# Pairs 5 to 11 of a gated linear attention with an MLP behind it: y laid out by tokens and turned by DMA, q and k turned in four transfers a pair, and a new order of all steps

## The chip, the cores and the metric

The kernel runs on one core of one Trainium2 chip. Its five engines have short names in the profile: PE is TensorE (PEld is its weight load), DVE is VectorE, ACT is ScalarE, POOL is GpSimd and SP is SyncE, which here only issues DMA transfers. The metric is the time of one execution on the device in microseconds (us). All times of the kernel before are from three runs and from one profiled execution.

## The reference, cut to what matters

First a gated linear attention, for 4 batches of 8 heads, 768 tokens each and 48 elements a head, then an MLP over all 3072 tokens with the activation h * cos(h):

```python
f = 1 / (1 + exp(-f_logit))                                  # all inputs (4, 8, 768, 48)
for t in range(S):
    state = f[:, :, t, :, None] * state + einsum('bhd,bhe->bhde', k[:, :, t], v[:, :, t])
    y[:, :, t] = einsum('bhd,bhde->bhe', q[:, :, t], state)
x = y.transpose(0, 2, 1, 3).reshape(3072, 384)
h = x @ w_in                                                 # w_in (384, 2048)
out = (h * cos(h)) @ w_out                                   # w_out (2048, 384)
```

## The kernel before, in words

**Pairs.** The attention is done in chunks of 128 tokens, and two chunks of a batch make a pair: 12 pairs, three to a batch, so pairs 0, 3, 6 and 9 begin a batch with an empty state. A pair's inputs f, k, q and v come in with tokens on the partitions (two neighbouring tokens to a partition, counted by e). Each pair runs these steps, with the pair's number in the name: `ex`, `ln`, `fx`, `fy` (ACT, logarithm of the gate), `qa`, `ka`, `ad` (POOL or DVE, one token folded into its neighbour), `cum` (PE, sums along the chunk), `eb`, `ei` (ACT, their exponentials), `qm` and `km` (q and k times these, into the tile `qk`), `vb` and `vt` (copies of v), then

- `tq`, `tk`: q and k are turned so that their elements lie on the partitions. In pairs 0 to 4 PE turns them (L435) and DVE or ACT copies the result out as `qkt`. In pairs 5 to 11 (`TURN_QK`) there is one DMA transpose for each half of the heads (L424), issued by SP: two a pair, 128 x 1024 elements each.
- `sc` (PE, L456): scores of q against k; `am` (DVE, L461): masked and copied to `am`.
- `ps` (PE, L479): k times v; `st` and `sz` (DVE): the carried state.
- `y` and `yi` (PE, L531): masked scores times v, and q times the carried state. They are made with the 384 outputs on the partitions, in strips of 32, so that the result is already the transposed x that the MLP reads: 32 matmuls of 32 columns of weights and 128 moving columns for `y`, and 24 for `yi` (12 in the first pair of a batch).
- `xe.0`, `xe.1` (ACT or DVE, L197): the two chunks of y copied from PSUM to the tile `x`.

**MLP.** Unit 0 and unit 1 are the two chunks of pair 0, and unit n + 1 is pair n, 256 tokens wide. A unit has steps `h` (PE, L579; h7.21 is unit 7, column block 2, half 1), `co` (ACT, the cosine), `g` (DVE, the product, L561), then for each 128 rows of the output four steps `o` (PE, L595), `ot` (copy) and `out` (DMA).

**Weights.** Eight transfers `w0.0` to `w0.3` (w_in) and `w1.0` to `w1.3` (w_out) of 768 KB, each cast to bfloat16 by a step `wc` on POOL or ACT.

**Order.** The order of all steps is written out by hand in the string `ORDER`: each word is a step, the letter of its engine (T PE, S ACT, V DVE, G POOL, Y SP) and the buffers that it takes. Every engine does its steps in this order, so a step that waits holds up all steps of its engine behind it; SP's queue is one list for loads, transposes and outputs. Steps `zf` are matmuls of zeros that keep PE busy in the beginning; other steps that begin with z clear buffers.

Of the kernel before, what the change touches and what calls it, by code (L numbers as in the profile page):

```python
# [38 lines left out]
fx0.0:S ei0.1:S0 fx0.1:S ei0.0:S ka0.0:V f1.1:Y1 km0.0:G0 f1.0:Y ex1.1:S ka0.1:V zf10:T2 zf11:T2
zf12:T2 zf13:T2 zf14:T2 zf15:T2 zf16:T2 zf17:T2 tk0.0:T2 eb0.1:S0 ex1.0:S ln1.1:S1 ln1.0:S fx1.0:S  # L40
q0.1:Y0 q0.0:Y v0:Y0 fx1.1:S eb0.0:S qa0.1:V zqk.1:V qm0.1:V vb0:S0 f3:Y2 k1.1:Y1 km0.1:V qa0.0:V
zf18:T3 cum1.1:T3 zf19:T4 zf20:T4 zf21:T4 tq0.1:T0 cum1.0:T1 qm0.0:G zsz.2:G eb1.0:S1 vt0.3:S2
k1.0:Y ei1.0:S0 ex3:S zf22:T4 zf23:T4 zf24:T4 zf25:T4 zf26:T4 ps0.1:T4,5 ps0.0:T tk0.1:T v1:Y1 f2:Y0
qkt0.1:V0 eb1.1:S ln3:S0 ei1.1:S ka1.0:G q1.0:Y0 tq0.0:T ka1.1:G km1.1:G0 zvt.1:G vt0.0:S ad3:G1
vt0.1:G q1.1:Y vb1:S1 qkt0.0:V1 vt0.2:G zsz.1:G ex2:S w0.1:Y0 w0.0:Y1 k3:Y0 q3:Y1 w0.3:Y2 ln2:S1
vt1.2:S1 fy3:S zf27:T6 zf28:T6 zf29:T6 zf30:T6 zf31:T6 zf32:T6 sc0.0:T0 sz0.01:V2 sz0.00:V w0.2:Y3
ad2:G0 vt1.0:G km1.0:V vt1.3:G wc0.1:G am0.0:V0 zf33:T6 zf34:T6 yi0:T4 sc0.1:T2 am0.1:V1 st0.11:V
sz0.11:V3 wc0.0:G k2:Y1 zf35:T6 zf36:T6 zf37:T6 zf38:T6 ps1.1:T6,7 tk1.0:T0 ps1.0:T zf39:T1 zf40:T1
zf41:T1 cum3:T1 fy2:S ei3:S0 fx3:S ka3:G eb3:S2 vt1.1:S fx2:S km3.0:G1 qa3:G qm3.0:G km3.1:G qm3.1:G
w1.0:Y0 qa1.0:V st0.10:V qa1.1:V qm1.0:V wc0.2:G ka2:G q2:Y2 tk1.1:T2 zf42:T3 zf43:T3 y0:T3 tq1.0:T  # L50
xe0.1:S0 sz0.10:V st1.00:V st1.01:V qm1.1:V v2:Y1 zf44:T5 zf45:T5 zf46:T5 zf47:T5 zf48:T5 tq1.1:T
cum2:T1 sz1.00:V1 qkt1.0:V0 eb2:S0 xe0.0:S ei2:S1 qkt1.1:V1 km2.0:G0 km2.1:G zf49:T5 sc1.0:T4
sz1.01:V zf50:T0 zf51:T0 sc1.1:T2 h0.01:T0 st1.11:V sz1.11:V2 am1.1:V0 wc1.0:G qa2:G zf52:T6 zf53:T6
h0.00:T co0.0:S0 qm2.1:G am1.0:V1 h1.01:T2 h1.00:T co1.0:S1 y1:T6,4 yi1:T g0.0:V1 xe1.1:V1 st1.10:V
qm2.0:G vb2:G1 sz1.10:V g1.0:V4 w1.2:Y3 xe1.0:S tk3.0:T5 h2.01:T0 tq3.0:T w1.3:Y0 qkt3.0:V0 v3:Y0
f4:Y0 h2.10:T6 h2.00:T sc3.0:T4 tq3.1:T2 tk3.1:T h2.11:T wc1.2:G wc1.3:G vt2.1:G1 wc0.3:S vb3:G0
co2.0:S1 am3.0:V0 g2.0:V2 h2.20:T4 h2.21:T h0.11:T0 co2.1:S0 qkt3.1:S1 co2.2:S1 sc3.1:T2 w1.1:Y3
g2.1:V am3.1:V1 g2.2:V h0.10:T h1.11:T6 h1.10:T h2.30:T2 tk2.1:T4 tk2.0:T5 co0.1:S0 co1.1:S2 g0.1:V
g1.1:V h2.31:T o2.0:T0 co2.3:S0 tq2.1:T vt3.2:G2 vt3.1:G tq2.0:T o0.0:T1 o3.0:T6 o1.0:T7 qkt2.0:S2
vt2.0:S g2.3:V qkt2.1:V3 sc2.0:T2 ex4:S o3.2:T o0.2:T am2.0:V2 ln4:S1 ps2.0:T4 sc2.1:T2 vt2.3:G  # L60
ps2.1:T am2.1:V3 st2.01:V st2.00:V sz2.01:V1 sz2.00:V wc1.1:S f5:Y2 ex5:S ln5:S0 o1.2:T o2.3:T
o3.3:T o0.3:T o2.2:T q4:Y2 ps3.0:T4,5 ps3.1:T zsz.0:G vt2.2:G ad4:G0 yi2:T2,3 y2:T vt3.3:G sz3.01:V0
sz3.00:V o1.3:T cum4:T4 v4:Y0 vt3.0:G ad5:G0 fy4:S eb4:S0 st3.11:V fx4:S k4:Y1 fy5:S qa4:G qm4.0:G1
fx5:S ei4:S1 o0.1:T o2.1:T o3.1:T xe2.0:V1 st3.10:V sz3.10:V1 qm4.1:G sz3.11:V xe2.1:V ot2:V0
h3.00:T2 o1.1:T cum5:T0 ei5:S0 eb5:S2 k5:Y0 h3.01:T ot0:V1 vb4:G0 ka4:G y3:T4,5 yi3:T q5:Y1 h3.10:T0
h3.11:T co3.0:S0 xe3.0:V0 xe3.1:V ot1:V2 ot3:V3 co3.1:S2 g3.0:V4 h3.21:T4 h3.20:T co3.2:S1 h4.21:T6
h4.20:T g3.1:V ka5:G km4.0:G co4.2:S0 km4.1:G vt4.1:G2 qa5:G h4.11:T2 h4.10:T g3.2:V co4.1:S2
h4.31:T0 k6:Y2 qm5.1:G0 h4.30:T vt4.0:G vt4.2:G km5.1:G f6:Y1 v5:Y0 v6:Y1 f7:Y0 tq4.0:T4 tq4.1:T5
out3:Y tk4.0:T tk4.1:T co4.3:S1 g4.2:V2 h3.31:T6 h3.30:T qkt4.1:S0 qkt4.0:V1 g4.1:V o5.1:T4 co3.3:S0
o5.2:T o5.0:T o4.1:T5 g4.3:V g3.3:V ps4.1:T0,1 ps4.0:T st4.01:V st4.00:V sc4.1:T2 sc4.0:T6 am4.1:V0  # L70
am4.0:V1 sz4.00:V0 sz4.01:V qm5.0:G vt4.3:G st4.10:V tq5.1:Y2 sz4.10:V2 o5.3:T o4.2:T km5.0:G o4.0:T
o4.3:T ex6:S ln6:S0 vb6:G0 ad6:G0 ex7:S cum6:T2 y4:T3,6 tq5.0:Y3 yi4:T ot5:S3 st4.11:V sz4.11:V
# [30 lines left out]
h9.20:T0 h9.21:T g9.0:V g9.1:V h10.10:T4 tq10.1:Y1 co9.2:S2 out7:Y g9.2:V h10.00:T2 h10.11:T
h10.20:T6 vt11.3:S1 co10.1:S1 g10.1:V4 h10.01:T co10.0:S2 o16.1:T0 h10.21:T o16.0:T g10.0:V o16.2:T
o16.3:T sc10.0:T2 co10.2:S1 out13:Y ot16:S3 g10.2:V sc10.1:T4 ps11.1:T1 vt11.0:G vt10.3:G2 ps11.0:T
qa11:G vt11.1:S qm11.1:G st11.01:V tq11.1:Y2 sz11.01:V2 am10.0:V0 am10.1:V1 h10.31:T6 o17.3:T0
# [611 lines left out]
```

## Time and profile before

| | |
|---|---|
| median of 3 runs | 183.1 us (183.05 to 183.54) |
| span of the profiled execution | 180.9 us |
| PE, PEld busy | 172.6, 123.9 us |
| DVE, ACT, POOL busy | 134.6, 130.7, 109.2 us |
| bytes moved by DMA | 33.93 MB |

The span runs from the first to the last instruction of the profiled execution. Its own time is this span of 180.9 us and what lies around it, which the span does not show; the median of the runs is 2.2 us above the span. Busy times of PE are of pipelined matmuls that overlap, so the distance from the start of one matmul to the start of the next, as the chain of waits and the timeline give it, is what one costs.

### The profile page before, as it was taken

The page shows a single profiled execution, that of the slowest core. Times are in us where ns is not written, and L with a number is a line of the kernel's source. Part 1 is how long each engine was busy: PE and PEld are TensorE (multiplying, and loading weights), DVE is VectorE, ACT ScalarE, POOL GpSimd, SP SyncE. Part 2 cuts the span into 40 slices and gives each one's busy share as a digit, 9 for nine tenths or more (in the row PEclk, how much of TensorE's full clock was granted, in tenths as well). Part 3 has the DMA queues.
Part 4 walks back from the last instruction along what each step waited for, and adds up shares of the span by engine and source line. Part 5 has one row for each costly group of instructions (what it writes and reads, how often), then busy time and mean ns, then how long its engine had stood idle before and what let it go on. Part 6 is the DMA issues. An engine that isn't in the chain of part 4 may idle for free.

```text
span 180.9 us, 5814 instructions
## 1 busy us (share of the span) xinstructions
PE 172.6 (95%) x2460; PEld 123.9 (69%) x2464; DVE 134.6 (74%) x206; ACT 130.7 (72%) x187; POOL 109.2 (60%) x139
## 2 busy tenths in 40 slices
PE   7899789999999999999999999999999999999992
PEld 2455467785668977778667886658788767787651
DVE  5259988897595988897999697689888894356260
ACT  3985987777878899989997899769768452473221
POOL 4229899999969986989665977890798000000000
PEclk9999999999999999999999999999999999999999
DMA  5999999999999944986899999559927500110313
GB/s 149 261 261 276 343 320 341 250 318 284 301 265 233 274 83 123 252 210 145 122 180 308 173 267 278 124 131 251 203 92 182 100 4 0 43 47 4 130 43 131
DMA packets 72282, 33.93 MB, mean 188 GB/s; under 512 B 65344, under 2 KB 70720, under 8 KB 72256
## 3 DMA queue, kind: packets, MB, share of 16 engines
q1 hardware_dynamic: 71584, 33.27, 75.7%
q8 instruction: 19, 0.31, 0.7%
q10 hardware_dynamic: 672, 0.30, 0.6%
q14 instruction: 7, 0.06, 0.1%
HBM read 25.17 MB, written 4.72 MB: 165 GB/s over the span
## 4 chain that ended last, share of the span: by engine, by line
PE 81%; DMA 7%; ACT 3%; DVE 3%; SPq 2%; issue 1%; ACTq 0%
PE ps L595 35%; PE ps L579 33%; PE ps L531 5%; DMA f<-in_f_logit_dram 4%; PE ps L456 4%; DMA v<-in_v_dram 3%; SPq L296 2%; PE ps L479 2%; DVE g L561 1%; PE ps L435 1%; PE ps L374 1%; DVE am L461 1%; PE ps L264 1%; ACT f L344 0%; ACT f L329 0%
## 5 line engine op out<-in xcount | busy, mean ns | idle before, releaser
L561 DVE TENSOR_TENSOR g<-ps,co 128x1024 bf16<-128x1024 f32 x48 | 57.4, 1220 | 18.0 <-ACT co L584 16.7
L595 PE MATMUL ps<-w_out_bf,g 128*128 128x384 bf16 x384 | 68.9, 326 | 0.0
L579 PE MATMUL ps<-x,w_in_bf 128*128 128x256 bf16 (+1 forms) x624 | 68.1, 264 | 0.5 <-DVE x L197 0.4
L584 ACT ACTIVATE co<-ps,halfpi 128x1024 bf16<-128x1024 f32 x48 | 52.7, 1113 | 19.8 <-PE ps L579 19.5
L579 PEld LDWEIGHTS <-w_in_bf 128*128 128x128 bf16 x624 | 56.3, 98 | 9.2 <-DVE x L197 0.6
L595 PEld LDWEIGHTS <-g 128*128 128x128 bf16 x384 | 36.1, 98 | 21.4
L461 DVE TENSOR_TENSOR am<-ps,pmask 128x1024 bf16<-128x1024 f32 x24 | 28.7, 1218 | 5.2 <-PE ps L456 4.9
L404 POOL TENSOR_TENSOR qk<-k,bi 128x384 bf16<-128x384 f32 x22 | 22.0, 1008 | 5.4 <-ACT bi L391 4.7
L404 POOL TENSOR_TENSOR qk<-q,b 128x384 bf16<-128x384 f32 x21 | 20.8, 1000 | 2.7 <-DVE q L338 2.1
L197 POOL COPY vt<-vb 64x384 bf16<-64x384 bf16 x33 | 16.7, 507 | 1.6
L264 PE MATMUL ps<-zero 128*128 128x512 bf16 x50 | 14.6, 412 | 1.5 <-DVE zero L203 1.2
L503 DVE TENSOR_TENSOR sz<-ps,b 64x192 bf16<-64x192 f32 x40 | 14.1, 354 | 2.5 <-PE ps L479 1.6
L363 POOL TENSOR_TENSOR sp<-ls 128x384 bf16<-128x384 f32 x10 | 10.3, 1028 | 7.8 <-ACT ls L333 6.1
L341 POOL TENSOR_TENSOR q<-f,q 128x384 f32<-128x384 f32 x10 | 10.0, 998 | 8.0 <-DMA q<-in_q_dram 5.8
L329 ACT ACTIVATE f<-f 128x768 f32<-128x768 f32 (+1 forms) x14 | 10.4, 746 | 4.4 <-DMA f<-in_f_logit_dram 4.4
L497 DVE TENSOR_TENSOR ps<-ps,sz 64x192 f32<-64x192 f32 x32 | 11.7, 367 | 2.2 <-PE ps L479 1.1
L351 POOL TENSOR_TENSOR k<-k,f 128x384 f32<-128x384 f32 (+1 forms) x12 | 11.1, 931 | 3.4 <-DMA k<-in_k_dram 3.4
L197 ACT COPY ot<-ps 128x384 f32<-128x384 f32 (+1 forms) x14 | 6.1, 453 | 8.7 <-PE ps L595 8.7
L197 ACT CAST x<-ps 128x384 bf16<-128x384 f32 x12 | 5.5, 479 | 6.0 <-PE ps L531 6.0
L456 PE MATMUL ps<-qkt 48*64 48x128 bf16 (+1 forms) x304 | 8.7, 218 | 1.1 <-ACT x L197 0.8
L197 DVE CAST x<-ps 128x384 bf16<-128x384 f32 x12 | 6.4, 553 | 4.1 <-PE ps L531 3.9
L264 PEld LDWEIGHTS <-zero 128*128 128x128 bf16 x54 | 4.8, 103 | 5.9 <-issue 1.9
(64 smaller groups left out, 167.2 us busy)
## 6 DMA issues: line engine op xcount, KB each, us to landing
v<-in_v_dram SPq DMA_DIRECT2D x12, 384.0 KB, 5.9
out_dram<-ot SPq DMA_DIRECT2D x22, 192.0 KB, 2.3
f<-in_f_logit_dram SPq DMA_DIRECT2D x10, 384.0 KB, 6.0
...
```

The source lines that it names most:

```text
L197: (nc.scalar.copy if e == "ACT" else eng(e).tensor_copy)(out=o, in_=i)
L264: G.step(f"zf{i}", ("PE",), lambda e, dump=dump: nc.tensor.matmul(dump.ap, lhsT=zero[:, 0:128], rhs=zero, start=True, stop=True), writes=[ ...
L351: eng(e).tensor_mul(out=w.ap[:, :, 0, :], in0=w.ap[:, :, 0, :], in1=t.ap[:, :, 0, :])
L404: G.step(f"{nm}{n}.{u}", ("POOL", "DVE") if cut else ("POOL",), lambda e, u=u, j=j, src=src, dec=dec: eng(e).tensor_mul(out=qkp[u][j].ap[: ...
L456: nc.tensor.matmul(o[t0:t1, r, 2 * a + g, :].rearrange("p (e n) -> p e n", e=2), lhsT=wide[s, t0 // 64, :] if turned else wide[s].rearrang ...
L461: G.step(f"am{n}.{u}", ("DVE",), lambda e, u=u, sc=sc: nc.vector.tensor_mul(out=am[u].ap.rearrange("p r b n -> p (r b) n"), in0=sc.ap.rear ...
L497: nc.vector.tensor_add(out=view()[s], in0=view()[s], in1=S0.ap[s, :, r, :])
L503: eng(e).tensor_mul(out=new.ap[s, :, r, :].rearrange("p (u a) n -> p u a n", u=2), in0=view()[s].rearrange("p (u a) n -> p u a n", u=2), i ...
L561: nc.vector.tensor_mul(out=o.rearrange("p b (n e) -> p b n e", e=2), in0=ph.ap.rearrange("p (b e n) -> p b n e", e=2, n=64), in1=co.ap.rea ...
L579: nc.tensor.matmul(ph.ap[:, i * T:(i + 1) * T].rearrange("p (g t) -> p g t", t=C), lhsT=w_in_bf[:, kk, f0:f0 + 128], rhs=xa[:, :, kk, :], ...
L584: G.step(f"co{m}.{j}", ("ACT",), lambda e, ph=ph, co=co: nc.scalar.activation(out=co.ap, in_=ph.ap, func=AF.Sin, bias=halfpi), reads=[ph], ...
L595: nc.tensor.matmul(po.ap[:, 0:DM], lhsT=gT.ap[:, j, i * C:(i + 1) * C], rhs=w_out_bf[:, j, :], start=(po.first and j == 4 * s), stop=(po.f ...
```

## The change

The kernel's steps for pairs 0 to 4 compute what they computed. In pairs 5 to 11:

- `y` and `yi` are made with tokens on the partitions (`inner_t`, `inter_t`): 16 matmuls of 128 columns of weights (`am`) and 48 moving columns (`vt`), and 8 (4 in the first pair of a batch) of 128 columns of weights (`qkt`) and 96 moving columns (the state).
- `xe` copies the chunk to a new tile `xr` (three buffers), and a new step `tx`, a DMA transpose of 128 x 384 elements on SP's queue, writes it to `x`: two a pair.
- `tq` becomes four DMA transposes a pair, each of 64 partitions of `qk`, so that q lies in `qkt` as the weights of `inter_t` need it. For this `qm` is written in another order, by two POOL instructions of 128 x 192 elements where there was one of 128 x 384.
- `ORDER` is new as a whole. Four more `zf` steps are in it.

```diff
+TURN_X = range(5, 12)
 SLOTS = {"f": 3, "k": 3, "q": 3, "v": 3, "sp": 3, "ls": 2, "b": 3, "bi": 3, "qk": 3, "vb": 3, "vt": 3, "qkt": 5, "am": 4,
-         "sz": 4, "x": 4, "g": 5, "co": 4, "ot": 4}
+         "sz": 4, "x": 4, "xr": 3, "g": 5, "co": 4, "ot": 4}
-ZEROS = 54
+ZEROS = 58
...
+        def scaled(e, u, j, src, dec):
+            o, d = qkp[u][j].ap, dec.ap[:, 0:HB].rearrange("p (h d) -> p h d", d=D)
+            if j == 1 or n not in TURN_QK:
+                eng(e).tensor_mul(out=o[:, :, :, 0:D], in0=swap(src.ap), in1=d[:, None].broadcast_to([128, 2, 4, D]))
+                return
+            for a in range(2):
+                h = slice(2 * a, 2 * a + 2)
+                eng(e).tensor_mul(out=o[:, a, :, 0:D].rearrange("p (e r) d -> p e r d", e=2), in0=swap(src.ap[:, h]),
+                                  in1=d[:, None, h].broadcast_to([128, 2, 2, D]))
...
             if turned:
-                G.step(f"tq{n}.{u}", ("SP",), lambda e, u=u: nc.sync.dma_start_transpose(
-                    out=qkt[u].ap.rearrange("p (b n) -> p b n", n=C),
-                    in_=qk.ap[:, u].rearrange("p j e h d -> p (j e h d)")),
-                    reads=[qkp[u][0], qkp[u][1]], writes=[qkt[u]])
+                for g in range(2):
+                    G.step(f"tq{n}.{u}{g}", ("SP",), lambda e, u=u, g=g: nc.sync.dma_start_transpose(
+                        out=qkt[u].ap[:, 512 * g:512 * g + 512].rearrange("p (b n) -> p b n", n=64),
+                        in_=qk.ap[64 * g:64 * g + 64, u].rearrange("p j e h d -> p (j e h d)")),
+                        reads=[qkp[u][0], qkp[u][1]], writes=[qktg[u][g]])
                 continue
...
+        def inner_t(e):
+            for g in range(2):
+                for h in range(H):
+                    nc.tensor.matmul(py[g].ap[:, D * h:D * h + D], lhsT=am[h // 4].ap[:, h % 2, h % 4 // 2 * 2 + g, :],
+                                     rhs=vt.ap[:, H * g + h, 16:16 + D], start=(py[g].first and h == 0),
+                                     stop=(py[g].final and h == H - 1))
+
+        def inter_t(e):
+            for g in range(2):
+                if before[g] is not None:
+                    for i in range(H // 2):
+                        nc.tensor.matmul(py[g].ap[:, 2 * D * i:2 * D * i + 2 * D],
+                                         lhsT=turn(i // 2, 0)[:, i % 2, g].rearrange("p e n -> p (e n)"),
+                                         rhs=before[g].ap[:, i].rearrange("p r d -> p (r d)"),
+                                         start=(py[g].first and i == 0), stop=(py[g].final and i == H // 2 - 1))
...
+            if laid:
+                xr = Val(xrS)
+                G.step(f"xe{n}.{g}", ("ACT", "DVE"), lambda e, g=g, xr=xr: copy(e, xr.ap, py[g].ap[:, 0:DM]),
+                       reads=[py[g]], writes=[xr])
+                G.step(f"tx{n}.{g}", ("SP",), lambda e, g=g, xr=xr: nc.sync.dma_start_transpose(
+                    out=xg[g].ap, in_=xr.ap), reads=[xr], writes=[xg[g]])
+                continue
```

Of the new order, four places that the prediction speaks of. The first transfers, before and after (f0.0 is ACT's, the others SP's):

```
before  f0.1 f0.0 k0.0 k0.1 f1.1 f1.0 q0.1 q0.0 v0 f3 k1.1 k1.0 v1 f2 q1.0 q1.1 w0.1 w0.0 k3 q3 w0.3 w0.2 k2 w1.0 q2 v2 w1.2 w1.3
after   f0.0 f0.1 v0 q0.1 f1.1 k0.0 k0.1 k1.1 f1.0 q0.0 q1.1 f3 v1 f2 q1.0 k1.0 w0.1 k3 w0.0 q3 w0.2 w0.3 w1.2 k2 q2 w1.0 v2 v3
```

PE from the last steps of pair 1 on, without zf:

```
before  y0 tq1.0 tq1.1 cum2 sc1.0 sc1.1 h0.01 h0.00 h1.01 h1.00 y1 yi1 tk3.0 h2.01 tq3.0 h2.10 h2.00 sc3.0 tq3.1 tk3.1 h2.11
after   tk1.0 sc1.1 tq1.0 cum3 cum2 sc1.0 y0 yi1 y1 yi0 h0.01 h0.00 h1.00 h1.01 tk3.0 h2.00 tq3.1 tk3.1 tq3.0 h2.11
```

In the order after, DVE from the end of pair 1's loads: km1.0, qkt1.1, st1.00, st1.01, am1.1, sz1.00, sz1.01, am1.0, st1.11, xe0.0, xe1.0, xe0.1; ACT: wc0.0, co0.0.

The steps of pair 7 around its turn, and the end:

```
after   ... yi7:T y7:T xe7.1:V tx7.1:Y xe7.0:V ot9:V tx7.0:Y ...   PE from y7 to h8.21: h6.01 h6.31 h6.30 h7.31 h7.20 h7.30 h7.10 h7.21
before  ... o23.1:T ot23.0:S out23.0:Y ot23.1:S out23.1:S
after   ... o22.3:T ot22.0:S out22.0:S ot22.1:S out22.1:Y
```

More of the change, by code (lines that the diff above doesn't have):

```diff
@@ L39 @@
[L39 to L72, printed above, removed]
@@ L103 @@
[L103 to L106, printed above, removed]
-h10.30:T vt10.2:G vt10.0:G o17.2:T o17.0:T o17.1:T vt10.1:S co10.3:S1 vt11.2:S ot17:S1 g10.3:V
-yi10:T4,5 y10:T qm11.0:G tq11.0:Y3 sc11.0:T6 sc11.1:T2 xe10.1:S2 zvt.0:V st11.00:V xe10.0:V o18.0:T0
@@ new lines @@
+zf18:T3 zf19:T3 zf20:T3 zf21:T3 zf22:T3 zf23:T3 zf24:T3 zf25:T3 cum1.1:T3 ei0.0:S0 ei0.1:S eb0.1:S1
+ei1.1:S1 eb1.1:S0 zsz.0:V ka0.0:V km0.0:V0 zf26:T0 zf27:T0 zf28:T0 zf29:T0 zf30:T0 zf31:T0 tk0.0:T3
+qm0.1:G k1.1:Y0 km0.1:V zf32:T0 zf33:T0 zf34:T0 zf35:T0 tk0.1:T5 f1.0:Y ex1.0:S q0.0:Y zsz.3:G
+qa0.0:V zvt.1:G ln1.0:S tq0.1:T qkt0.1:V0 q1.1:Y1 qa1.1:V ps0.1:T1,6 zf36:T0 zf37:T0 sc0.1:T4
+cum1.0:T0 eb0.0:S ei1.0:S qm0.0:V tq0.0:T qkt0.0:S1 fx1.0:S am0.1:V0 f3:Y1 ex3:S ln3:S0 eb1.0:S
+fx3:S ka1.1:G zsp.2:G ps0.0:T sz0.00:V0 sz0.01:V st0.11:V st0.10:V sz0.10:V3 zf38:T7 zf39:T7 zf40:T7
@@ new lines @@
+zf41:T7 sc0.0:T2 am0.0:V3 vt0.1:G v1:Y1 sz0.11:V f2:Y2 km1.1:G1 tk1.1:T1 vb1:G0 zf42:T7 ps1.1:T7,4
+q1.0:Y ex2:S vt1.0:G0 k1.0:Y ln2:S1 fx2:S vt1.2:S vt1.1:S qa1.0:V ad3:G0 qm1.1:V zf43:T5 zf44:T5
+zf45:T5 zf46:T5 zf47:T5 zf48:T5 zf49:T5 zf50:T5 zf51:T5 zf52:T5 tq1.1:T ka1.0:G km1.0:V qkt1.1:V2
+zsz.1:V zf53:T5 zf54:T5 zf55:T5 zf56:T5 zf57:T5 ps1.0:T st1.00:V tk1.0:T3 sc1.1:T0 qm1.0:G tq1.0:T
+cum3:T5 ad2:G1 cum2:T6 vt1.3:S qkt1.0:S4 w0.1:Y0 wc0.1:G vt0.0:G st1.01:V am1.1:V1 sz1.00:V1 eb3:S2
+fy3:S ei3:S2 sz1.01:V eb2:S1 ei2:S1 sc1.0:T2 am1.0:V2 y0:T0,1 yi1:T5,7 st1.11:V y1:T yi0:T xe0.0:V2
@@ new lines @@
+xe1.0:V0 xe0.1:V sz1.11:V2 h0.01:T2 k3:Y2 ka3:G w0.0:Y1 wc0.0:S h0.00:T co0.0:S2 h1.00:T0 h1.01:T
+km3.0:G0 tk3.0:T6 km3.1:G st1.10:V sz1.10:V xe1.1:V h2.00:T4 q3:Y0 qa3:G g0.0:V3 qm3.1:G tq3.1:T7
+tk3.1:T qkt3.1:V3 qm3.0:G tq3.0:T co1.0:S3 g1.0:V1 h2.11:T2 h2.10:T qkt3.0:S4 sc3.0:T6 am3.0:V1
+fy2:S w0.2:Y2 wc0.2:G co2.1:S0 h2.01:T h2.21:T0 co2.0:S3 g2.1:V2 g2.0:V h2.20:T co2.2:S2 h0.10:T6
+g2.2:V w0.3:Y4 wc0.3:G h0.11:T co0.1:S1 h1.11:T2 h1.10:T sc3.1:T4 am3.1:V0 w1.2:Y0 k2:Y1 g0.1:V
+wc1.2:G h2.30:T0 h2.31:T o2.2:T4 co1.1:S0 g1.1:V o3.2:T5 ka2:G km2.1:G2 tk2.1:T6 q2:Y2 qa2:G qm2.1:G
@@ new lines @@
+st7.11:V vb8:G0 yi7:T0,1 f11:Y1 y7:T xe7.1:V2 tx7.1:Y1 xe7.0:V1 ot9:V1 tx7.0:Y tq8.01:Y2 v10:Y1
+ka9:G km8.1:G km9.0:G1 qm8.1:G sz7.11:V out8:Y v11:Y0 f10:Y2 tq8.00:Y q11:Y1 tq8.10:Y0 out7:Y out9:Y
+eb9:S2 qm9.1:G km9.1:G tq9.11:Y4 tq8.11:Y tq9.10:Y qm9.0:G vb10:G2 tq9.01:Y3 h6.01:T co6.0:S2
+tq9.00:Y h6.31:T6 h6.30:T co6.3:S0 h7.31:T0 g6.0:V h7.20:T2 h7.30:T co7.3:S3 vt8.1:G0 g6.3:V
+vt10.0:G2 vt9.0:G h7.10:T4 h7.21:T co7.2:S1 h8.21:T6 h8.20:T co8.2:S0 g7.3:V3 h7.11:T co7.1:S2
+h7.00:T0 h7.01:T co7.0:S3 g7.2:V g8.2:V0 h8.11:T2 h8.10:T co8.1:S1 o10.3:T6 o11.2:T7 o11.3:T o11.0:T
@@ new lines @@
+o19.0:T h11.30:T4 sz11.01:V h11.11:T0 h11.10:T vt11.0:G g11.2:V2 o19.2:T y11:T2,3 yi11:T ot19:V1
+out19:Y xe11.0:S1 xe11.1:V0 o16.1:T ot16:V0 tx11.1:Y2 h11.31:T co11.1:S0 g11.1:V out16:Y o15.0:T6
+o15.3:T co11.3:S2 g11.3:V h11.01:T2 h11.00:T co11.0:S2 o15.1:T o15.2:T ot15:V3 tx11.0:Y h12.20:T0
+h12.21:T o20.1:T5 h12.00:T6 g11.0:V h12.01:T co12.0:S2 g12.0:V3 co12.2:S1 g12.2:V o21.0:T4 h12.31:T2
+h12.30:T o20.0:T co12.3:S0 o21.3:T h12.11:T6 h12.10:T co12.1:S1 o21.2:T g12.3:V o21.1:T ot21:S1
+out21:Y out12:Y o20.3:T o23.3:T2 o23.2:T o23.0:T o22.0:T0 g12.1:V o23.1:T o20.2:T ot20:S0 ot23.1:V1
@@ L117 @@
+ot23.0:V out23.1:Y out15:Y o22.2:T out23.0:S out20:Y o22.1:T o22.3:T ot22.0:S2 out22.0:S ot22.1:S
+out22.1:Y
 """
@@ L401, in pair @@
         qkp = [[qk.part(lambda a, u=u, j=j: a[:, u, j]) for j in range(2)] for u in us]
+        def scaled(e, u, j, src, dec):
[7 more added lines that the diff above has]
+                                  in1=d[:, None, h].broadcast_to([128, 2, 2, D]))
         for u in us:
             for j, (nm, src, dec) in enumerate((("qm", qh[u], bth[u]), ("km", kh[u], bih[u]))):
-                G.step(f"{nm}{n}.{u}", ("POOL", "DVE") if cut else ("POOL",), lambda e, u=u, j=j, src=src, dec=dec: eng(e).tensor_mul(
-                    out=qkp[u][j].ap[:, :, :, 0:D], in0=swap(src.ap),
-                    in1=dec.ap[:, 0:HB].rearrange("p (h d) -> p h d", d=D)[:, None].broadcast_to([128, 2, 4, D])),
-                    reads=[src, dec], writes=[qkp[u][j]])
+                G.step(f"{nm}{n}.{u}", ("POOL", "DVE") if cut else ("POOL",), lambda e, a=(u, j, src, dec): scaled(e, *a),
+                       reads=[src, dec], writes=[qkp[u][j]])
         vb, vt = Val(vbS), Val(vtS)
@@ L418, in pair, with turn @@
         qkt = [Val(qktS), Val(qktS)]
+        qktg = [[w.part(None) for _ in range(2)] for w in qkt]
         turned = n in TURN_QK
-        order = "p (j e a g n) -> p j a g e n" if turned else "p (j a g e n) -> p j a g e n"
-        qkv = lambda u: qkt[u].ap.rearrange(order, j=2, a=2, g=2, e=2)
+        order = "p (j a g e n) -> p j a g e n"
+        def turn(u, j):
+            if not turned:
+                return qkt[u].ap.rearrange(order, j=2, a=2, g=2, e=2)[:, j]
+            half = qkt[u].ap.rearrange("p (g j b n) -> p g j b n", g=2, j=2, b=4)[:, :, j]
+            return half.rearrange("p g (e a) n -> p a g e n" if j else "p g (a e) n -> p a g e n", e=2)
         for u in us:
             if turned:
-                G.step(f"tq{n}.{u}", ("SP",), lambda e, u=u: nc.sync.dma_start_transpose(
-                    out=qkt[u].ap.rearrange("p (b n) -> p b n", n=C),
-                    in_=qk.ap[:, u].rearrange("p j e h d -> p (j e h d)")),
-                    reads=[qkp[u][0], qkp[u][1]], writes=[qkt[u]])
+                for g in range(2):
[3 more added lines that the diff above has]
+                        reads=[qkp[u][0], qkp[u][1]], writes=[qktg[u][g]])
                 continue
```

102 lines of the change are left out of this document (59 added, 43 removed).

## The prediction

> **What bounds the kernel now.** I read the page first, then busy time by windows, then the chain of waits.
>
> ```profile
> span 180.9 us, 5814 instructions
> ```
>
> ```profile
> 18.00:34.00 16.00, 13.53 (x234) 9.70 (x232) 14.00 (x25) 13.09 (x21) 15.06 (x17) 1.00 1.08 331
> 34.00:60.00 26.00, 26.00 (x380) 19.34 (x380) 20.31 (x30) 21.18 (x26) 23.44 (x28) 1.00 1.11 271
> 60.00:100.00 40.00, 40.00 (x704) 29.75 (x702) 35.55 (x52) 36.54 (x53) 31.67 (x40) 1.00 0.84 188
> 100.00:140.00 40.00, 40.00 (x537) 30.75 (x535) 32.02 (x43) 32.48 (x43) 30.70 (x39) 1.00 0.82 188
> 140.00:177.00 37.00, 37.00 (x436) 26.22 (x434) 22.05 (x27) 14.72 (x19) 0.00 (x0) 1.00 0.16 47
> ```
>
> The columns are the stretch, its length, then busy time of PE, PEld, DVE, ACT and POOL, the granted clock, the DMA share and GB/s. From 34 us PE is busy without a gap, at full clock (1.00). Before that it is not: 13.53 of 16 us, and part of this is zeros.
>
> ```profile
> 33.92 2.14 PE ps L579 x24
> 36.06 0.33 PE ps L456 x8
> ...
> 63.08 0.89 PE ps L435 x16
> 63.97 1.31 PE ps L579 x12
> ...
> 71.67 0.08 PE ps L380 x4
> 71.75 0.90 PE ps L531 x56
> 72.64 0.76 PE ps L595 x4
> ...
> 80.29 0.65 PE ps L595 x4
> 80.94 0.90 PE ps L531 x56
> ...
> 98.10 1.51 PE ps L531 x100
> ...
> 122.08 0.90 PE ps L531 x56
> ...
> 129.57 0.73 PE ps L531 x44
> ...
> 146.34 0.90 PE ps L531 x56
> ...
> 155.08 0.90 PE ps L531 x56
> ...
> 177.84 0.33 ACT ot L197
> ```
>
> These rows of the chain are start, length and count. From 33.92 us (h2.11) to the last matmul the chain is PE alone, so there each us of PE work taken out, or of waiting put in, is a us of the end. The profiled execution's span of 180.9 us stands 2.2 us below the median of 183.1 us; I make the sum as differences and put it on 183.1. 0.3% of it, 0.55 us, is about what a measurement of this kernel can tell from no change.
>
> **Term 1: y and yi of pairs 5 to 11 on PE.** The old form is the six L531 rows from 80.94 on: 0.90 four times, 1.51 (pairs 6 and 7 together) and 0.73, 5.84 us for 368 matmuls. What follows pays too: four L595 take 0.76 us behind L531 and 0.65 us elsewhere, 0.11 us in six places, 0.66. Together 6.5 us. The new form is 112 matmuls with 48 moving columns and 48 with 96, all with 128 x 128 weights like the MLP's, so that the 0.11 goes. No row has these shapes. The nearest with such weights are L380 (2 columns: 0.08/4 = 20 ns), L435 (128 columns: 0.89/16 = 56 ns) and L579 (256 columns: 1.31/12 = 109 ns), so about 0.42 ns a column above 128. I take 25 ns for 48 columns, near L380 since the line from L435 gives 22, and 42 ns for 96: 2.8 + 2.0 = 4.8 us. **Term: -1.7 us.** Bounds: at 20 and 42 ns -2.3, and if all went at L435's 56 ns, 9.0 us, so +2.5.
>
> Here a rule is to be weighed. Start to start the 16 matmuls of L435 are 56 ns apart although each loads new weights, and such a load has this row:
>
> ```profile
> L435 PEld LDWEIGHTS <-qk 128*128 128x128 bf16 x80 | 4.9, 97 | 2.9 <-DVE qk L404 1.8 <-POOL qk L404 0.5
> ```
>
> So a load of 97 ns lies beside the matmuls and does not pace them. The Trainium skill (TensorE: Matmul & The Clock Gate, "Back-to-back issue gap") says that in a stream of weight loads and matmuls the spacing is set by both, about 81 ns at 128 columns. By that figure the 160 new matmuls are an estimated 13.0 us, and the term +6.5; the trace, with 56 ns, disagrees.
>
> **Term 2: the first 34 us.** Here ORDER changes most.
>
> ```profile
> 19.21 0.34 DVE L338 SCALAR_TENSOR_TENSOR q<-f,q 128x192 f32<-128x192 f32 x1
> 22.06 1.27 DVE L197 COPY qkt<-ps 128x1024 bf16<-128x1024 bf16 x2
> 22.18 2.87 POOL L197 CAST w_in_bf<-g 128x1536 bf16<-128x1536 f32 x2
> 23.36 0.36 DVE L503 TENSOR_TENSOR sz<-ps,b 64x192 bf16<-64x192 f32 x1
> 24.70 1.28 ACT L584 ACT_TABLE_LOAD   x1
> 24.95 2.36 DVE L461 TENSOR_TENSOR am<-ps,pmask 128x1024 bf16<-128x1024 f32 x2 [0.43 <-PE ps L456]
> 26.75 1.11 ACT L584 ACTIVATE co<-ps,halfpi 128x1024 bf16<-128x1024 f32 x1 [0.78 <-PE ps L579]
> 27.95 1.23 DVE L561 TENSOR_TENSOR g<-ps,co 128x1024 bf16<-128x1024 f32 x1 [0.65 <-issue]
> 29.10 0.55 DVE L197 CAST x<-ps 128x384 bf16<-128x384 f32 x1
> 29.46 1.48 ACT L197 CAST w_in_bf<-g 128x1536 bf16<-128x1536 f32 x1
> ```
>
> h2.11 needs the PSUM tile that g0.0 frees. Two chains lead there in the new order. By DMA: POOL cast w0.1 and w0.0 back to back from 22.18, so w0.0 had landed by about 23.6; the same transfers stand ahead of it after, and k3 besides, 384 KB, 1.2 us at 331 GB/s: 24.8. Then its cast (now on ACT) 1.48, the table 1.28, co0.0 1.11, g0.0 1.23: 29.9 us. By DVE: pair 1's last load has landed by the row at 19.21 (the same bytes stand ahead of it after); ka1.0 on POOL about 0.6, then km1.0 0.5, one qkt 0.64, two st 0.8, am1.1 1.2, two sz 0.7, am1.0 1.2, st1.11 0.4, xe0.0 0.5: h0.01 at 25.7 us, before co0.0 is due at 27.6. So h2.11 at 29.9, against 33.92. But less PE work stands ahead of it after: sc3.0 (0.33), h2.01 and h2.10 (0.65 each) come later, 1.6 us. Gain 33.9 - 29.9 - 1.6 = 2.4. Behind h2.11 DVE has qkt3.1, g1.0, am3.0 and three g, 6.7 us, until h2.30 may start, and PE has 6.6 us of work until there: 0.1 lost. **Term: -2.3 us.** Bounds: -3.5 if the table comes before w0.0's cast ends, and +0.5 if v0, now second in the queue, holds pair 0's k and q back into that DVE chain.
>
> **Term 3: x through DMA.** What is new on the path: y ends, xe copies, tx is issued by SP and lands, then h may start.
>
> ```profile
> L424 SPq DMA_TRANSPOSE qkt<-qk x14: 1232/1248/2691, 65.1 to 140.0; - x14
> ...
> DMA to landing us min/median/max: 3.0/3.2/5.1
> ```
>
> A 128 x 1024 transpose holds SP 1.25 us and lands 1.95 us later. For 128 x 384 the issue lies between 3/8 of this (0.47) and the same 1.25. Pair 7, where both copies are DVE's: 0.55 + 0.55 + 0.47 + 1.95 = 3.5 us; with 1.25 each 0.55 + 1.25 + 1.25 + 1.95 = 5.0; with the longest landing 0.55 + 1.25 + 5.1 = 6.9. Between y and the unit's first h the new order puts PE work (h and o 0.65 each, ps 0.37) of 6.9, 6.1, 5.2, 6.8, 6.2, 5.8 and 5.2 us in pairs 5 to 11. So the wait is 0 at the lower end, and at 6.9 us 0 + 0.8 + 1.7 + 0.1 + 0.7 + 1.1 + 1.7 = 6.1 us. I take 0.47 by bytes, nearest the low end, and one or two late landings behind loads: **+0.6 us**. Bandwidth is there: 60 to 140 us leaves 0.16 and 0.18 of 40 us each, 13.6 us, and 14 x 96 KB at the 188 GB/s of those rows is 7.3.
>
> **The four tq.** The same bytes in twice the transfers: by bytes 0.62 us of SP each, nothing in sum; at 1.25 each 17.5 us more, and the 14 tx again 6.6 to 17.5. SP has no steady work in 60 to 140 us: its waits for POOL are what the transposes stand on. A tx that waits for its xe holds up what is queued behind it on SP: behind tx7.0 the tq of pair 8 and loads of pairs 10 and 11; behind tx11.1, out16, which waits for ot16, and only then tx11.0. The loads are two pairs early, so I put nothing. Of qm, POOL's price rises:
>
> ```profile
> L404 POOL TENSOR_TENSOR qk<-q,b 128x384 bf16<-128x384 f32 x21 | 20.8, 1000 | 2.7 <-DVE q L338 2.1
> ```
>
> ```profile
> 13.73 1.14 POOL L351 TENSOR_TENSOR k<-k,f 128x192 f32<-128x192 f32 x2 [2.06 <-DMA k<-in_k_dram]
> ```
>
> Two halves are 1.14 for 1.00, 14 times 0.14, 2.0 us, while POOL is busy 62.4 of 80 us: 0, and +2.0 if that slack is gone.
>
> A rule speaks against this part: the Trainium skill (DMA: Bandwidth & Descriptors, "Rules for kernel authors") says of two transfers to disjoint partition halves not to bother, since they serialize on the same 16 engines, and to use one. No row here shows half transfers; by it the split gains nothing and at worst doubles the issue.
>
> **Term 4: the end.** The last copies were ACT, ACT, then the issue; now ACT's issue of out22.0 stands between them.
>
> ```profile
> 178.20 0.36 ACTq L606 DMA_DIRECT2D out_dram<-ot  x1
> ```
>
> That is 0.36 and ACT's own wait for its copy: **+0.5 us** (0.3 to 0.8).
>
> The four zf more lie in PE's idle start: 0. **Sum: -1.7 - 2.3 + 0.6 + 0.5 = -2.9, so 180.2 us.** With the terms' nearer bounds (head -1.2 to -3.3, waits 0 to 1.5) this case alone goes from 178.6 to 182.2.
>
> **The rivals.**
> *x comes late (slower).* SP's issue does not shrink with the bytes and the landings queue behind loads, so that the time from y to x is near 6.9 us: term 3 is 6.1 instead of 0.6, 185.7 us. It decides from about 6.3 us on, where the waits sum to 3.5. For it: the longest landing of 5.1 and the longest issue of 2.69. Against: the median of 3.2 with 2.7 times the bytes.
> *SP becomes the bound (slower).* All 42 transposes at 1.25 us are 52.5 us of 80, 35 more than now, beside loads that hold SP 0.4 to 2.7 us each: units wait for tq and loads. If 8 us of the 35 find no room, 188.2 us.
> *Weights pace the narrow matmuls (slower).* At the 97 ns of the PEld row 160 are 15.5 us, term 1 is +9.0: 190.9 us. L435 and L380 speak against it.
> By the skill's 81 ns it would be an estimated 188.4 us.
> *The head gains nothing.* If PE's wait only moves behind h2.11, where DVE and PE are even to 0.1 us, term 2 is 0: 182.5 us, and with pair 0 held back by v0, 183.0.
>
> **How the numbers follow.** Forecast 0.62; x late 0.15; SP 0.05; weights 0.04; head without gain 0.14, of which 0.05 lie below 182.55, 0.08 within 0.55 us and 0.01 above. Faster 0.67, same 0.08, slower 0.25. The range for 8 in 10 runs from 178.0, a little under the forecast's own low end for the two far bounds of term 2 and term 1, to 184.8, which takes in the head's case and the milder half of the late x.
>
> **What would show it.** PE's rows of the new y at about 0.74 us a pair with 0.65 for the L595 behind (term 1); h2.11 near 30 us and PE full from there (term 2); tx landing in about 2.5 us and no wait of PE for x above 0.5 us in a pair (term 3); tq issues near 0.6 us; out22.0 between two copies of ACT at the end. I am wrong if PE idles after 34 us for DMA x or DMA qkt, or if the y rows are above 1.0 us.

## The result, and the profile after

The changed kernel takes **195.8 us** (195.33 to 196.32), the kernel before 183.2: a ratio of 1.067 (95% interval 1.063 to 1.072), 12.6 us slower where 2.9 us faster was forecast. The profiled execution has a span of 193.7 us, 12.8 above before. From the page of the changed kernel (span, granted PE clock in 40 slices, the chain's shares by engine):

```profile
span 193.7 us, 5477 instructions
PEclk9999999999999999999988999999999999999998
PE 46%; DMA 16%; DVE 11%; SPq 9%; POOL 7%; ACT 6%; issue 4%; ACTq 0%; POOLq 0%; DVEq 0%
```

Before, PE held 81% of the chain and DMA 7%. The windows of the changed kernel (columns as in the prediction) show where PE no longer works through:

```profile
18.00:34.00 16.00, 12.57 (x246) 9.28 (x244) 13.76 (x25) 12.85 (x20) 14.97 (x15) 1.00 1.08 326
34.00:60.00 26.00, 25.74 (x385) 19.17 (x383) 21.18 (x31) 23.38 (x31) 19.72 (x23) 1.00 1.07 271
60.00:100.00 40.00, 37.40 (x547) 27.73 (x546) 32.61 (x43) 33.87 (x45) 32.98 (x46) 1.00 0.94 192
100.00:140.00 40.00, 36.26 (x474) 26.37 (x472) 29.47 (x44) 27.97 (x40) 24.74 (x34) 0.96 0.89 173
140.00:190.00 50.00, 48.71 (x468) 35.56 (x467) 31.26 (x39) 21.16 (x25) 7.95 (x13) 1.00 0.31 77
```

Waits of PE that were not there before (who waits and for what; then their sum in us, how many, the longest):

```profile
PE ps L476 <- DMA qkt<-qk: 4.4, 3, 2.2
...
PE ps L625 <- DMA x<-xr: 1.7, 3, 0.7
```

Matmuls are pipelined, so waits and busy times do not add up to the loss. I therefore took from the trace when each PE step starts, and from the order how much PE work stands ahead of it, each form at its gapless spacing (h 0.655 us, o 0.65, the new y 0.43). The difference is the time that PE has lost by then. The column "neither" is an experiment below.

| PE time lost (us) at the start of | before | after | "neither" |
|---|---|---|---|
| h3.01 (55 to 58 us) | 20.8 | 22.6 | 22.7 |
| sc6.1 (92 us) | 21.2 | 23.9 | 23.9 |
| sc8.0 (114 to 122 us) | 21.3 | 29.8 | 24.1 |
| sc10.1 (142 to 150 us) | 21.4 | 33.6 | 24.9 |
| end of the last o | 21.7 | 35.6 | 25.2 |

The work itself fell from 155.9 to 154.3 us. So the 12.8 us of span are -1.6 for the work, +1.8 in the head, +0.9 until sc6.1, +5.8, +3.7 and +1.7 in the three stretches after it, and 0.5 behind the last o. The loss is in the middle, where the DMA transposes are. Their rows in the changed kernel (issue in ns min/median/max; then us to landing):

```profile
L444 SPq DMA_TRANSPOSE qkt<-qk x28: 1195/1262/2328, 66.7 to 153.5; - x28
...
DMA to landing us min/median/max: 2.6/3.2/5.7
...
L598 SPq DMA_TRANSPOSE x<-xr x14: 1177/1202/2170, 80.4 to 171.7; - x14
...
DMA to landing us min/median/max: 2.3/3.2/5.4
```

A transpose of half the elements (L444), or of three eighths (L598), holds SP as long as the 128 x 1024 one did, 1.25 us. So 42 of them are, at these medians, some 52 us of SP where there were 17.5. What that does to the queue, first in a row of POOL, then in SP's timeline (start, length):

```profile
86.83 1.15 POOL L416 TENSOR_TENSOR qk<-q,b 128x192 bf16<-128x192 f32 x2
```

```profile
85.04 1.20 SPq L444 DMA_TRANSPOSE qkt<-qk  x1
86.29 0.57 SPq L302 DMA_DIRECT2D k<-in_k_dram  x1
86.98 4.00 SPq L444 DMA_TRANSPOSE qkt<-qk  x3
91.03 1.06 SPq L652 DMA_DIRECT2D out_dram<-ot  x2
92.14 0.45 SPq L302 DMA_DIRECT2D k<-in_k_dram  x1
92.68 2.65 SPq L444 DMA_TRANSPOSE qkt<-qk  x2
```

The last scaled q that tq7.00 and tq7.01 read is done at 87.98 us. SP issues without a break, with pair 6's four halves, outputs and a load ahead in the queue, and comes to them at 92.68 and 94.06: 4.7 and 6.1 us late. Before, 10 of the 14 were issued 0.03 us after their input. The chain goes on:

```profile
94.06 4.68 DMA qkt<-qk
98.74 0.04 issue
98.79 0.36 PE ps L476 x12
99.15 0.76 PE ps L641 x4
99.90 0.62 PE ps L570 x16
```

The scores of pair 7 (sc7.0) wait 2.2 us for the first of the two landings, and after the wait the granted clock falls. The landings themselves, 5.7 and 4.7 us after the issue where the median is 3.2, are part of this wait:

```profile
95.90:98.40 2.50, 0.29 (x33) 0.18 (x26) 0.00 (x0) 1.26 (x3) 1.95 (x2) 1.00 0.73 111
98.40:103.50 5.10, 4.96 (x71) 3.06 (x72) 3.79 (x7) 1.53 (x4) 0.06 (x1) 0.67 0.92 210
```

In those 5.1 us the clock is 0.67, and steps of about 3.0 us of work take 5.0: the wait costs nearly double. Waits repeat, at full clock, at sc8.1 (0.7 us) and sc9.0 (1.5), whose transposes are issued 9.4 and 10.2 us after their input, and where units wait for x at h7.31, h9.31, h11.20 and h12.20 (1.0, 0.5, 0.5 and 0.7 us; the first of these ends with a copy on DVE that waited for tx6.0 to free its buffer of `xr`). These are idle times of PE; counted from start to start, as the expectations below have them, most are 0.1 to 0.2 us longer.

### The profile page after: what moved, and what is told of

Its sections match the earlier page's. It is cut to its first block, busy times and chain, and to the rows that moved or that the text cites. A ratio compares the mean times of both kernels' runs of the same rounds, so it can differ in the third digit from the quotient of the medians.

```text
span 193.7 us, 5477 instructions
## 1 busy us (share of the span) xinstructions
PE 176.4 (91%) x2260; PEld 125.8 (65%) x2260; DVE 140.6 (73%) x210; ACT 130.2 (67%) x182; POOL 111.7 (58%) x154
## 2 busy tenths in 40 slices
DMA packets 78552, 35.28 MB, mean 182 GB/s; under 512 B 71616, under 2 KB 76992, under 8 KB 78528
## 4 chain that ended last, share of the span: by engine, by line
PE 46%; DMA 16%; DVE 11%; SPq 9%; POOL 7%; ACT 6%; issue 4%; ACTq 0%; POOLq 0%; DVEq 0%
PE ps L625 23%; PE ps L641 15%; DMA qkt<-qk 6%; DMA x<-xr 5%; SPq L302 4%; SPq L444 3%; DVE am L481 3%; DMA g<-in_moe_w_in_dram 3%; DVE g L607 3%; DMA f<-in_f_logit_dram 2%; ACT co L630 2%; POOL qk L416 2%; POOL qk L412 2%; DVE ps L517 2%; DVE sz L523 2%
## 5 line engine op out<-in xcount | busy, mean ns | idle before, releaser
L641 PE MATMUL ps<-w_out_bf,g 128*128 128x384 bf16 x384 | 69.9, 328 | 0.0
L641 PEld LDWEIGHTS <-g 128*128 128x128 bf16 x384 | 36.0, 98 | 21.3 <-issue 0.6
L412 POOL TENSOR_TENSOR qk<-k,bi 128x384 bf16<-128x384 f32 x21 | 20.8, 1000 | 3.4 <-issue 2.4
L270 PE MATMUL ps<-zero 128*128 128x512 bf16 x58 | 15.7, 410 | 1.2 <-DVE zero L208 1.2
L416 POOL TENSOR_TENSOR qk<-q,b 128x192 bf16<-128x192 f32 x28 | 15.8, 591 | 0.2
L202 DVE COPY ot<-ps 128x384 f32<-128x384 f32 (+1 forms) x16 | 8.3, 528 | 10.5 <-PE ps L641 10.3
L476 PE MATMUL ps<-qkt 48*64 48x128 bf16 (+1 forms) x304 | 10.3, 226 | 5.5 <-DMA qkt<-qk 4.4
L357 POOL TENSOR_TENSOR k<-k,f 128x384 f32<-128x384 f32 (+1 forms) x13 | 11.7, 902 | 4.8 <-DMA k<-in_k_dram 4.8
L476 PEld LDWEIGHTS <-qkt 48*64 48x64 bf16 (+1 forms) x304 | 6.4, 105 | 10.8 <-DMA qkt<-qk 5.4
L202 POOL CAST vb<-v 128x768 bf16<-128x768 f32 x9 | 7.4, 823 | 4.7 <-DMA v<-in_v_dram 4.6
L270 PEld LDWEIGHTS <-zero 128*128 128x128 bf16 x58 | 5.4, 104 | 7.0 <-issue 1.9
```

The lines of the kernel that those rows point to most:

```text
L202: (nc.scalar.copy if e == "ACT" else eng(e).tensor_copy)(out=o, in_=i)
L270: G.step(f"zf{i}", ("PE",), lambda e, dump=dump: nc.tensor.matmul(dump.ap, lhsT=zero[:, 0:128], rhs=zero, start=True, stop=True), writes=[ ...
L412: eng(e).tensor_mul(out=o[:, :, :, 0:D], in0=swap(src.ap), in1=d[:, None].broadcast_to([128, 2, 4, D]))
L416: eng(e).tensor_mul(out=o[:, a, :, 0:D].rearrange("p (e r) d -> p e r d", e=2), in0=swap(src.ap[:, h]), in1=d[:, None, h].broadcast_to([12 ...
L476: nc.tensor.matmul(o[t0:t1, r, 2 * a + g, :].rearrange("p (e n) -> p e n", e=2), lhsT=wide[s, t0 // 64, :] if turned else wide[s].rearrang ...
L641: nc.tensor.matmul(po.ap[:, 0:DM], lhsT=gT.ap[:, j, i * C:(i + 1) * C], rhs=w_out_bf[:, j, :], start=(po.first and j == 4 * s), stop=(po.f ...
```

## The experiments

Theory: an SP issue of about 1.2 us per transpose, whatever its size, makes SP's in-order queue late. Rivals: the way of x alone, the bytes on the DMA engines, POOL's price for the split q, and the new order itself.

**The split alone** (old order, old y):

```diff
-tq5.1:Y2
+tq5.10:Y2 tq5.11:Y        # and so for all 14
```

> The old order and the old y, q and k of pairs 5 to 11 turned in four half transfers instead of two. SP theory (each transpose holds SP about 1.24 us whatever its size, and the in-order queue runs late): 14 transposes more, 17.4 us of SP; the second half lands 1.25 us or more later, and in the kernel before the scores of pairs 6, 7 and 9 start only 0.4 to 1.6 us after their transpose lands, so PE waits some 2 to 5 us: 185 to 188 us. If the split costs nothing, as the prediction had it: 183 us.

Measured: 188.3 us, ratio 1.026 (1.022 to 1.031). The split costs 5.1 us where the prediction had nothing. The Trainium skill's advice against two transfers to disjoint partition halves (DMA: Bandwidth & Descriptors, "Rules for kernel authors"), weighed in the prediction, holds here. That the halves share the 16 engines, the reason given there, does not show as the cause: the DMA share in the two windows from 60 to 140 us is 0.75 and 0.85, against 0.84 and 0.82 before.

**Taking the transposes out of the changed kernel.** Three runs: without those of x, with one half instead of two, and both.

```diff
-xe6.0:S1 tx6.0:Y3         # no tx: the copy writes x itself
+xe6.0:S3
-tq6.10:Y4 ... tq6.11:Y    # one half: PE reads it twice
+tq6.1:Y4
```

> The changed kernel without the 14 transposes of x: the copy out of PSUM writes x itself, with the tokens still on the partitions, so this leaves out the turning of x. SP theory: the waits of PE for x (about 3.3 us) go, and SP is 17 us freer, so part of the waits for qkt goes too: 187 to 190 us. If x's way alone is the cause: 183 to 184. If the qkt transposes alone are the cause: 192 or more.

> The changed kernel with one half transfer of q and k for each four heads instead of two; PE reads the first half in the place of the second, so this leaves out the turning of the second half. SP theory: 17.5 us of SP less, the waits for qkt (2.3, 1.0, 1.6 us and the slow clock behind the first) go, those for x mostly stay: 186 to 190 us. If x's way is the cause: 193 or more.

> Both of the last two: no transposes of x, and one half transfer instead of two, so 14 transposes in all as in the kernel before, each of half the bytes; it leaves out the turning of x and of the second half of q and k. What is left is the new order and the new y. SP theory: all stalls after 60 us go; 183.2 less 1.6 for the y on PE, plus about 2 for the head, plus 0.4 for the end: 184 us. If the new order stalls for other reasons (POOL, DVE): 187 or more.

Measured: 189.4 us (1.034, 1.030 to 1.039), 187.1 us (1.022, 1.019 to 1.024) and 184.9 us (1.009, 1.007 to 1.012). So 10.8 of the 12.6 us go with the transposes. Taken off the changed kernel, those of x are worth 6.4 us and the second halves 8.6; neither alone is the cause, as expected of one shared queue. The windows of the run with neither:

```profile
60.00:100.00 40.00, 39.55 (x596) 29.36 (x594) 35.49 (x49) 36.19 (x51) 34.03 (x48) 1.00 0.90 209
100.00:140.00 40.00, 39.83 (x499) 31.32 (x497) 33.14 (x48) 31.22 (x41) 31.37 (x45) 1.00 0.50 113
```

PE is nearly gapless there, at full clock. What is left, 1.8 us above before though PE has 1.6 less to do, is the new order's: the same steps in the old order (182.1 us, the first run under "Term 1 and POOL" below) take 2.8 us less. In the run without x's transposes the longest wait that was left came another way, as its chain shows:

```profile
99.44 6.04 DMA out_dram<-ot
105.48 0.03 issue
105.51 0.02 DVEq L200
105.53 0.04 issue
105.58 0.56 DVE ot L200
```

DVE waits for an output that has not left, since its copy needs that buffer; the steps behind it on DVE are late, and PE's h waits 1.9 us. SP's lateness reaches PE by outputs too.

**SP's time by itself.** In the run with neither, 28 small transposes for which no one waits, then the same 28 in full size:

```diff
+for i in range(28):
+    G.step(f"tt{i}", ("SP",), lambda e, i=i: nc.sync.dma_start_transpose(out=tout[:, i], in_=tin[0:64]))
```

> The run that has neither (184.9 us), with 28 transposes of 64 x 128 of a tile of zeros put on SP at the places where the transposes of x and the second halves stood. No one waits for them, and they move 16 KB each, 0.45 MB in all. Leaves out what that run left out. If it is SP's time per transpose: 1.2 us each, SP late as before, and all comes back but the waits for x: 188 to 192 us. If it is the bytes: 185 us, with issues of 0.2 us or so.

> The run with 28 transposes that no one waits for (190.1 us), now each with the full size of the one in whose place it stands: 14 of 64 x 1024 and 14 of 128 x 384, 3.2 MB instead of 0.45. If SP's time per transpose is all: 190 us, within 1. If the bytes count beside it: 192 to 195 us.

Measured: 190.1 us (1.038, 1.035 to 1.041) and 191.5 us (1.045, 1.042 to 1.047). The small ones in the trace:

```profile
L265 SPq DMA_TRANSPOSE tout<-tin x28: 1088/1226/2151, 69.1 to 166.4; - x28
```

16 KB take 1.23 us of SP, as 256 KB did. SP's time, with hardly any bytes, gives 5.2 us of the 10.8; the bytes add 1.4; the other 4.2 come with what PE waits for.

**Fewer and larger transposes, the same work.** First 21 instead of 42: for each pair two of 64 x 2048 and one of 128 x 768.

```diff
-out=qkt[u].ap[:, 512 * g:512 * g + 512]..., in_=qk.ap[64 * g:64 * g + 64, u]...
+out=both.ap[:, 1024 * g:1024 * g + 1024]..., in_=qk.ap[64 * g:64 * g + 64]...
```

> The changed kernel with the same work and the same bytes in 21 transposes instead of 42: for each pair two of 64 x 2048 (both groups of heads together) and one of 128 x 768 for x. If it is SP's time per transpose that counts (1.24 us whatever the size), SP is 26 us freer, and what is left is near the run with 28 transposes (187.1 us) or a little under: 185.5 to 188 us, and the rows show issues near 1.25 us for the doubled sizes. If it is the bytes or the DMA engines that count: 194 us or more, and issues near 2.5 us.

Measured: 195.0 us (1.068, 1.065 to 1.071), a miss: no gain over the changed kernel, and a time that fits the bytes as the cause. The next two tell the two causes apart: they turn 128 partitions at once, with 28 and 21 transposes.

```diff
-for g in range(2): ...in_=qk.ap[64 * g:64 * g + 64, u]
+in_=qk.ap[:, u]
-lhsT=turn(i // 2, 0)[:, i % 2, g].rearrange("p e n -> p (e n)")
+lhsT=turn(i // 2, 0)[:, i % 2, g, x, :]      # x = 0, 1
-out=xg[g].ap, in_=xr.ap                      # from here the second of the two
+out=x.ap.rearrange("p g m n -> p (g m) n"), in_=xr.ap.rearrange("p g m -> p (g m)")
```

> The changed kernel with one transpose of 128 x 1024 for each four heads in the place of two of 64 x 1024: all the bytes and nothing left out, 28 transposes instead of 42. The matmuls of q on the state are doubled (two of 64 weight columns for one of 128), 48 more, 1.2 to 2.0 us of PE at 25 to 42 ns. If the count on SP's in-order queue is the cause: the 187.1 us of the run with 28 transposes and half the bytes, plus 1.2 to 2.0: 188.3 to 189.1. If the bytes on the DMA engines are the cause: 194 us or more.

> The run with one transpose of 128 x 1024 for each four heads, and x in one of 128 x 768 a pair instead of two of 128 x 384: 21 transposes, nothing left out. Against that run SP has 8.7 us less, x waits for both copies but for one issue only. If the count on SP is the cause: 186.5 to 188 us. If it is the bytes, or x's way: no less than that run.

Measured: 188.1 us (1.027, 1.025 to 1.028) and 186.8 us (1.019, 1.017 to 1.020). All bytes are moved (35.29 MB in the second run, 35.28 in the changed kernel, in about as many packets), and 21 transposes fewer give 9.0 us: the load on the DMA engines is a small part of what held the changed kernel back. The first stands 1.0 us above the run with half the bytes of q and k, which the doubled matmuls (1.2 to 2.0 us as estimated) more than account for. To find what held back 64 x 2048, two runs more. The first was to make each transpose wait for all eight heads (its declared reads became those of the whole pair), and moved the words of q and k to the later place:

> The run with 21 transposes that was fast (186.8 us: 14 of 128 x 1024, 7 of 128 x 768), changed in one thing: each transpose of q and k waits for the scaled q and k of all eight heads of the pair, and both stand at the later place in SP's queue, as the two of 64 x 2048 did in the run that stayed at 195.0 us. If that wait is what kept the 21 transposes there from gaining, 3 to 5 us come back or more: 190 us and up. If it was the size of the transposes (issues of 1.9 to 4.4 us): 186.8 to 188.

Measured: 186.7 us (1.021, 1.019 to 1.022). The wait did not come about: the transposes still started after what they read themselves, so this run shows only that the later place costs nothing. The second turns q of all eight heads in one transfer and k in the other:

```diff
-in_=qk.ap[:, u].rearrange("p j e h d -> p (j e h d)")
+in_=qk.ap[:, j].rearrange("p u e h d -> p (u e h d)")      # qk laid out with j ahead of u
```

> The last run did not put the wait in: its transposes still started once their own four heads were there (the first of pair 5 at 66.4 us, the pair's last scaled half at 68.5), so it showed only that the later place in SP's queue costs nothing. Here q of all eight heads is one transpose of 128 x 1024 and k of all eight the other, so that each must wait for both halves of the pair, with the same 21 transposes and bytes as in the runs of 186.8 and 195.0 us. If the wait for the whole pair kept 64 x 2048 from gaining: 190 us or more. If it was the shape (64 partitions, issues of 1.96 us in the median, 4.4 at the longest): 186.5 to 188.

Measured: 189.4 us (1.034, 1.030 to 1.037). The value lies between the two forecasts, so both seem to count: waiting for the whole pair, with the new layout of qk, costs 2.6 us against 186.8, and the run with 64 x 2048 stands 5.7 above this one. These 5.7 are not the shape's beyond doubt, since there each transpose also waits for q and k both, and 48 matmuls are fewer. The rows of q and k in the run with 64 x 2048, then in this one:

```profile
L444 SPq DMA_TRANSPOSE qk<-qk x14: 1244/1962/4447, 68.7 to 151.1; - x14
...
DMA to landing us min/median/max: 3.8/4.5/6.5
```

```profile
L444 SPq DMA_TRANSPOSE qk<-qk x14: 1233/1326/3222, 67.9 to 146.0; - x14
```

The same bytes from 64 partitions hold SP 1.96 us, from 128 partitions 1.33. In the run with 64 x 2048 SP issued 53.8 us between 60 and 140 us, 11.0 less than in the changed kernel, and PE still waited 6.1 us for q and k: a freer SP is not enough where each transpose starts and lands later.

**Term 1 and POOL by themselves**, in the old order with 14 transposes: the new y, then the old y.

```diff
-TURN_X = ()
+TURN_X = range(5, 12)     # without tx
```

> The order of the kernel before with the new y of pairs 5 to 11 on PE, one half transfer instead of two and no transposes of x (it leaves out the turning of x and of the second half of q and k). This is term 1 by itself, with the halved copies of q on POOL: if the term is right, 1.6 us under the kernel before, 181.6 us (181.0 to 182.2); if POOL's 2.0 us are not hidden, 183 or more.

> The last one with the old y: the order and y of the kernel before, 14 transposes, each of half the bytes, and the halved copies of q on POOL (it leaves out the turning of the second half of q and k). If POOL's slack hides the 2.0 us: 183.2 us, within 0.5; if not, up to 185. Against the run that has the split (188.3 us) it tells what is the 14 more transposes and what is POOL: the SP theory expects that nearly all of the 5.1 us are the transposes.

Measured: 182.1 us (0.995, 0.993 to 0.998) and 183.1 us (1.000, 0.998 to 1.001). POOL's two instructions for one cost nothing in the old order. The new y gains 1.0 us (0.4 to 1.2), less than the 1.6 of PE work; PE is busy 39.46 of the 40 us from 100 to 140 there, where before it was busy all of them.

**The head.** One step of the run with neither moved from DVE to POOL:

```diff
-km1.0:V
+km1.0:G
```

> The run that has neither (184.9 us), with one step of the head moved: km of pair 1's first half on POOL instead of DVE, where it took 1.35 us on the chain to the first h. If DVE's own work sets the head, as the rows of the changed kernel say: 0.9 to 1.3 us less, 183.6 to 184.0 us. If the head is set by the loads or by POOL: 184.9 or more.

Measured: 185.3 us (1.012, 1.008 to 1.015), no gain. The step on POOL pushed POOL's qm1.0 from 20.02 to 20.94 us, and DVE's other multiply (qm1.1), 0.95 us in the run with neither and 0.54 in the changed kernel, took as long as the one taken away:

```profile
20.04 1.35 DVE L409 TENSOR_TENSOR qk<-q,b 128x384 bf16<-128x384 f32 x1
```

No version tried beats the kernel before with all the work in it; the nearest are 186.7 and 186.8 us, and 182.1 us without the turning of x and of half of q and k bounds what the new y can give in the old order.

## Why the prediction was wrong

**The four tq: this step failed.** It took the issue by bytes, 0.62 us; it is 1.26. The rival "SP becomes the bound" had it right in kind and was given 0.05. It put 8 us of SP's 35 as not finding room; some 11 us came. Its 188.2 us is still 7.6 short, mostly by the head (4.1) and these stalls (2.6). What spoke for it was in the trace of before: SP's issues between 60 and 140 us sum to 51.4 us (14 transposes 21.1, 20 loads 18.9, 15 outputs 11.4), and 35 more are above 80. I had counted only SP's waits, and called that "no steady work". The sum points the way and does not give the size: the changed kernel issued only 64.8 us there, since 13 of its 42 transposes came after 140 us and outputs and loads took less. But from 66.7 to 129.4 us it issued with no pause above 0.8 us. In such a queue each transpose stands behind others: lateness of 4 to 10 us, where three scores before (sc6.1, sc7.0, sc9.1) started 0.4 to 1.1 us after their landing.

**Term 3: failed for the same reason.** It took tx at 0.47 us; it is 1.20, and the landing is 3.2 us in the median, as for 2.7 times the bytes. PE's waits for x are about 2.7 us, against 0.6 forecast and 6.1 in the rival. In pair 6 the larger part is the queue: the copies end at 101.42 us, the transposes are issued at 103.10 and 104.39, and land at 108.47 and 108.91. The last is issued 3.0 us late and lands 1.3 us later than the median would have it. (Two slips of the working moved nothing: at 6.3 us the waits sum to 3.0, not 3.5, and the longest load behind 60 us held SP 3.12 us, not 2.7.)

**Term 2: wrong, and outside its bounds.** The head loses 1.8 us instead of gaining 2.3. The step that failed is the DVE chain, h0.01 at 25.7 us; it came at 27.71. DVE and the chain of the changed kernel:

```profile
19.60 0.57 DVE L344 SCALAR_TENSOR_TENSOR q<-f,q 128x192 f32<-128x192 f32 x1
20.09 0.54 DVE L412 TENSOR_TENSOR qk<-q,b 128x384 bf16<-128x384 f32 x1
20.56 1.35 DVE L412 TENSOR_TENSOR qk<-k,bi 128x384 bf16<-128x384 f32 x1
...
22.63 0.22 DVE L236 MEMSET sz<- 128x192 uint32 x1
```

```profile
27.71 1.89 PE ps L625 x31
29.60 1.23 issue
30.83 1.11 PE ps L625 x17
```

km1.0 took 1.35 us where I put 0.5, and I left out qm1.1 (0.54) and a memset (0.22): 1.6 of the 2.0 us. Then PE stands 1.23 us for a cause that the profile does not show; such a stretch, 0.9 to 1.6 us, was in most runs with this head. So h2.11 came at 33.49 us where 29.9 was forecast.

**Term 1: right in size.** Rows of the changed kernel, pair 8:

```profile
131.72 0.40 PE ps L570 x16
132.12 0.19 PE ps L578 x4
```

The new y is 25 ns a matmul, as taken; the 96 columns are 42 to 45 where nothing holds them up (0.34 to 0.36 us for 8). Together 4.8 to 5.0 us, forecast 4.8; the run in the old order gained 1.0 of the 1.7 us. The rival that weights pace them falls. The 81 ns that the Trainium skill (TensorE: Matmul & The Clock Gate, "Back-to-back issue gap") states at 128 columns are not seen here: 16 matmuls of that width took 0.89 us in the kernel before, 56 ns each.

**Term 4: right.** 0.5 us behind the last o, with ACT's issue between two copies:

```profile
189.94 0.33 ACT ot L202
...
190.28 0.34 ACTq L652
...
190.66 0.32 ACT ot L202
```

POOL's split was hidden, as said, in the old order. Of the signs named for a wrong prediction PE's waits after 34 us for DMA qkt and for DMA x appeared; y rows above 1.0 us did not. The range ended at 184.8 us because the SP case, at 188.2 us, had been left outside it.
